# A spectral filter beside a gated MLP: the inverse transform's exchange is issued before its row and summed two pairs later, and the feature transform reads its low parts from a ninth tile

## The chip, the cores and the metric

The kernel runs on one core of a Trainium2 chip. The metric is the device time of one execution in microseconds (us), lower is better. One execution was taken by the hardware profiler; times inside it count from the start of its span. Engines: PE (matrix products, with PEld for its weight loads), DVE (vector), ACT (activations), POOL, and SP, whose queue issues every transfer here. Each engine takes its instructions in order.

## The reference

```python
x = A_x                                   # 1 x 2048 x 448, float32
xn = _layernorm(x, axis=-1)
X = jnp.fft.rfft2(xn, axes=(-2, -1))      # spectral branch
y = jnp.fft.irfft2(X * (w_r + 1j * w_i), s=(2048, 448), axes=(-2, -1))
gate = xn @ W_gate                        # 448 x 1792
up = xn @ W_up
h = gate * (gate > 0) * up                # gated branch
out = x + y + h @ W_down
```

## The kernel before, in words

All products run on PE in float16, each operand split into a high and a low part, so that one exact product costs three matmuls: high by high, high by low, low by high.

Tokens are held as 16 groups of 128 (`n2`), four groups to a chunk; chunks go in the order 0, 2, 1, 3. The 448 features are cut into four residues of 112. For a group, the normalized values stand in a tile `tt` of eight blocks of 128 columns: blocks 0 to 2 hold residues 0 to 2 with 16 values of residue 3 behind each; block 3 holds the last 64 values of residue 3, high part in its first half and low part in its second; blocks 4 to 6 hold the low parts of 0 to 2; block 7 gathers residue 3's high part, written by two POOL copies (`ln_copy`). The blocks are transposed into `Tq[q]`, for the first four groups by PE (`ln_tp`, `ln_ev`), for the others by one DMA transpose each (`ln_dma`).

**The gated branch** is the bulk of PE's work. Units `gu_unit` (L727, and half passes L734) make gate and up for 128 hidden columns by 512 tokens; `gu_post` brings them through ACT and DVE (`gu_relu` L764, `gu_times` L768, `gu_hi` L772, `gu_lo` L776); units `dn_mm` (L795) multiply by `W_down`, and `dn_post` (L801) adds to the result `xy`. Weights are scaled by a power of two found from a sum of squares (`w_sq` on ACT, `w_sum` an all-reduce on POOL, `w_scale`, then `w_hi` L677 and `w_lo` L681).

**The spectral branch** is a list of background steps (`bg`), dealt out between those units by a credit of DVE time. Forward: `f_dft` (L370) transforms a group over the features, `f_eo`, `f_x`, `f_lo` fold it, `f_sdft` (L412) transforms over 128 tokens with a table `fm`, and `stage2` to `stage4` finish over the 16 groups by DVE butterflies (L418 to L442). A real transform pairs each frequency with its mirror: `swap` sends the upper half of the partitions of two buffers to the lower half of an exchange tile `sw` and the lower half to the upper, by two transfers (L559, L560), and `pair` (L565, L566) adds or subtracts the tile. Three exchange tiles are used in turn. Then come the weights (`wmul`, from tiles `wf`), `turn`, and the inverse butterflies.

One frequency, partition 64 of the tiles, takes a separate way: `row_in` collects it into `row`, `row_hi` to `row_ev` transform it by two small products with `row_t`, and in the inverse half `i_swap` puts it back into partition 64 of the two buffers before it calls `swap`.

Inverse, for pair m = 0 to 7: `stage4`, `i_swap`, `i_pair`, `i_hi` and `i_lo` (L609, L615, into `vt`, two buffers), then for two groups each `i_sdft` (L625, table `im`), `i_pq` and `i_pqlo` (L631, L635, into `pgh`), `i_ddft` (L645) and `i_acc` (L650), which adds to `xy`; a group is stored (L807) when both branches have added to it. `i_sdft` and `i_ddft` share two PSUM banks `fx` with the other spectral products.

The order of the opening on every engine, up to the first chunk's hidden values and the first part of `W_down`, is written out by hand (`OPENING`, short names: `lo2` is `ln_lo` of group 2, `dm2` its `ln_dma`, `parW4` the all-reduce of weight tile 4). After it, each engine's order is set by a planner that simulates the program with priorities.

The lines that set the distance between exchange and sum: in the forward half

```python
if i0 < 8:
    add(bf[k0], stage4, k0, 1, "s3", "X")
if i0 > 1:
    add(1.26, pair, "X", ks[i0 - 2], 1)
if i0 < 8:
    add(0.0, swap, "X", k0)
```

and in the inverse half, for even half-steps t = 2m,

```python
if m < 8:
    add(bf[m], stage4, m, -1, "i3", "U")
if 0 <= m - 1 < 8:
    add(1.26, i_pair, m - 1)
    add(0.0, i_hi, m - 1)
if m < 8:
    add(0.0, i_swap, m)
```

Of the kernel before, what the change touches and what calls it, by code (L numbers as in the profile page):

```python
# [19 lines left out]
KC = 57  # L20
# [14 lines left out]
wloW0g1 lw lfd hh01 hh11 whiW1g0 st2 lh01 lh10 whiW1g1 hl01 wloW1g0 lw hl11 wsqW2g0 wloW1g1 lw ly0 ly4 ly8  # L35
ly12 lh11 wsqW3g0 st10 parW2 hp0 st14 wsqW3g1 gu1g0 st6 wdq0 parW3 wscW2 sqC wscW3 whiW2g0 rsC gu1g1 re0
wloW2g0 whiW3g1 tm0 whiW2g1 xn6 wsqW4g0 xn2 gu2g0 wloW2g1 hi2 re1 xn10 gh0 wloW3g1 whiW3g0 tm1 gu2g1 wdq1
wloW3g0 hi10 xn14 lo2 hi14 hi6 cp14 hp2 wsqW4g1 cp2 lo6 gu3g0 cp10 dm2 lo14 re2 parW4 wdq2 cp6 wscW4 tm2
whiW4g0 dm14 lo10 wdq4 gu3g1 wloW4g0 gh1 dm10 gl0 whiW4g1 gl1 dm6 gu4g0 re3 wloW4g1 wdq3 tm3 wdp gh3
# [30 lines left out]
def _fd_parts():  # L70

    names = [("h", r) for r in range(4)] + [("l", r) for r in range(4)] + [("x", 3)]
    off = {n: GW * i for i, n in enumerate(names)}
    for r in range(3):
        off["x", r] = GW * (9 + 2 * r)
    return off, GW * 15


# [8 lines left out]
def _constants():  # L87
    sc = 2.0 ** 10
    rows = _rows()
    kp = np.arange(KC)  # L90

    def dft(d):
        th = 2 * np.pi * ((np.outer(d, kp)) % D) / D
        return np.concatenate([np.cos(th), -np.sin(th)], axis=1) * sc

    off, width = _fd_parts()
    c_fd = np.zeros((128, width), np.float16)
    p = np.arange(128)
    in3 = (p < 48) | (p >= 64)
    d3 = 4 * np.where(p < 48, p, np.where(p < 64, 0, p - 16)) + 3  # L100
    for r in range(4):
        h, l = _split(dft(rows[r] if r < 3 else d3))
        keep = (p < 112 if r < 3 else in3)[:, None]
        c_fd[:, off["h", r]:off["h", r] + GW] = np.where(keep, h, 0)
        c_fd[:, off["l", r]:off["l", r] + GW] = np.where(keep, l, 0)
    for r in range(3):
        h, _ = _split(dft(rows[r]))
        c_fd[:, off["x", r]:off["x", r] + GW] = np.where((p < 112)[:, None], h, 0)
        c_fd[:, off["x", r] + GW:off["x", r] + 2 * GW] = np.where((p >= 112)[:, None], h, 0)
    h, _ = _split(dft(rows[3]))  # L110
    c_fd[:, off["x", 3]:off["x", 3] + GW] = np.where((p >= 64)[:, None], h, 0)
# [46 lines left out]
def tile_gfnet_reglu(ctx: ExitStack, tc: tile.TileContext, x, xr, wgu, wd, wf, wrow, ident, c_fd, c_fm, c_im, c_row, c_id,  # L158
# [19 lines left out]
    Tq = {q: mt([128, 8, 512], F16, f"T{q}") for q in CHUNKS}  # L178
# [9 lines left out]
    fd_off, fd_width = _fd_parts()  # L188
# [42 lines left out]
    fd_t = ft([128, fd_width], F16, "fd_t")  # L231
# [109 lines left out]
    def ln_dma(n2):  # L341
        q, j = n2 % 4, n2 // 4
        o = Tq[q][:, :, 128 * j:128 * (j + 1)]
        last["S"] = nc.sync.dma_start_transpose(o, tt[n2].rearrange("p a b -> p (a b)")).ins
# [18 lines left out]
    def f_dft(n2):  # L363
        q, j = n2 % 4, n2 // 4
        js = slice(128 * j, 128 * (j + 1))
        ps = fx()
        T = Tq[q]

        def mm(o, a, part, first=False):
            P.matmul(o, T[:, a, js], fd_t[:, fd_off[part]:fd_off[part] + (2 * GW if part in wide else GW)],  # L370
                     start=first, stop=True, skip_group_check=True)

        wide = [("x", r) for r in range(3)]
        p4 = ps[:, 0:4 * GW].rearrange("p (c w) -> p c w", c=4)
# [117 lines left out]
    def open_inv():  # L492
# [104 lines left out]
    def i_swap(m):  # L597
        for n in (m, m + 8):
            nc.sync.dma_start(cur["U", n][64:65].rearrange("p g c k -> p (g c) k"), row[8 * n:8 * n + 8, 0, :])
        swap("U", m)  # L600

# [217 lines left out]
    def ln_chunk(q):  # L819
# [14 lines left out]
    def fft_chunk(q):  # L834
        n = [q + 4 * j for j in (0, 2, 1, 3)]
        for t in range(10):
# [5 lines left out]
            for i, fn in steps + [(t - 1, f_eo), (t, f_dft)]:  # L842
# [4 lines left out]
                if fn is f_eo:  # L847
# [31 lines left out]
    add(0.0, lambda: nc.sync.dma_start(idc_t, c_id))  # L879
    ks = [0, 4, 2, 6, 1, 5, 3, 7]  # L880
# [161 lines left out]
    for c, q in enumerate(CHUNKS[:2]):  # L1042
# [114 lines left out]
def _arrays(A_x, A_w_r, A_w_i, B_W_gate, B_W_up, B_W_down):  # L1157
# [15 lines left out]
    wrow = wf[:, 64].reshape(16, 2, 4, 1, KC).repeat(2, axis=3).transpose(0, 2, 3, 1, 4).reshape(128, 2, KC)  # L1173
    wf = wf.reshape(2, 8, 128, 2, 4 * KC).transpose(1, 2, 3, 0, 4).reshape(8, 128, 16 * KC)
# [25 lines left out]
```

## Time and profile before

| | |
|---|---|
| median of 3 runs | 459.4 us (458.9 to 461.23) |
| the profiled execution | 459.03 us |
| its span | 457.2 us |
| PE busy | 440.9 us (96%) |
| DVE busy | 374.0 us (82%) |
| ACT, POOL busy | 177.6, 26.1 us |
| moved by DMA | 39.35 MB |

The span runs from the first to the last instruction; the 1.8 us by which the execution is longer lie around it. A group's idle time is that of its engine just before it, with what ended it; time that an engine off the chain sits idle costs nothing by itself.

### The profile page before, as it was taken

The page shows a single profiled execution, that of the slowest core. Times are in us where ns is not written, and L with a number is a line of the kernel's source. Part 1 is how long each engine was busy: PE and PEld are TensorE (multiplying, and loading weights), DVE is VectorE, ACT ScalarE, POOL GpSimd, SP SyncE. Part 2 cuts the span into 40 slices and gives each one's busy share as a digit, 9 for nine tenths or more (in the row PEclk, how much of TensorE's full clock was granted, in tenths as well). Part 3 has the DMA queues.
Part 4 walks back from the last instruction along what each step waited for, and adds up shares of the span by engine and source line. Part 5 has one row for each costly group of instructions (what it writes and reads, how often), then busy time and mean ns, then how long its engine had stood idle before and what let it go on. Part 6 is the DMA issues. An engine that isn't in the chain of part 4 may idle for free.

```text
span 457.2 us, 7054 instructions
## 1 busy us (share of the span) xinstructions
PE 440.9 (96%) x2618; PEld 220.3 (48%) x2618; DVE 374.0 (82%) x801; ACT 177.6 (39%) x363; POOL 26.1 (6%) x68
## 2 busy tenths in 40 slices
PE   7999999999999999999999999999999997989896
PEld 3544645544555444444444444444444454545464
DVE  5998798988759898999999997988886768665664
ACT  5996242522535573143224242642321341323220
POOL 2220030110000130000000000000000000000000
PEclk9999999999999999999999999999999999999999
DMA  7929992040002352350220210000002231121213
GB/s 257 355 49 288 309 260 57 10 108 1 1 24 94 106 173 80 83 161 1 83 81 1 69 55 0 1 0 0 2 3 80 67 91 44 38 93 53 94 53 115
DMA packets 36955, 39.35 MB, mean 86 GB/s; under 512 B 15878, under 2 KB 32184, under 8 KB 36920
## 3 DMA queue, kind: packets, MB, share of 16 engines
q1 hardware_dynamic: 36920, 38.89, 27.6%
q8 instruction: 20, 0.33, 0.3%
q14 instruction: 15, 0.12, 0.1%
HBM read 24.65 MB, written 3.67 MB: 62 GB/s over the span
## 4 chain that ended last, share of the span: by engine, by line
PE 78%; DVE 10%; DMA 7%; issue 2%; SPq 1%; ACT 1%; DVEq 0%; ACTq 0%
PE gu L727 45%; PE dn L795 23%; DMA sw<-y 5%; PE gu L734 3%; PE fx L370 3%; PE fx L412 2%; DVE vt L615 1%; DVE xy L801 1%; PE fx L645 1%; DMA y<-in_xr 1%; DVE g L768 1%; DVE y L565 1%; DVE y L566 1%; PE fx L625 1%; DVE xy L650 1%
## 5 line engine op out<-in xcount | busy, mean ns | idle before, releaser
L727 PE MATMUL gu<-T,wt 128*128 128x512 f16 (+1 forms) x1140 | 256.1, 375 | 0.0
L727 PEld LDWEIGHTS <-wt 128*128 128x128 f16 x1140 | 109.0, 98 | 129.6 <-issue 9.3
L795 PE MATMUL dn<-wdt,h 128*128 128x448 f16 x672 | 136.8, 352 | 1.4 <-DVE xy L801 1.4
L795 PEld LDWEIGHTS <-h 128*128 128x128 f16 x672 | 65.0, 98 | 61.7 <-issue 1.6
L764 ACT ACTIVATE g<-gu 128x512 f32<-128x512 f32 x56 | 33.3, 594 | 115.6 <-PE gu L734 81.6
L772 ACT ACTIVATE h<-g 128x512 f16<-128x512 f32 x56 | 34.9, 626 | 65.4 <-DVE g L768 65.3
L768 DVE SCALAR_TENSOR_TENSOR g<-gu,g 128x512 f32<-128x512 f32 x56 | 38.4, 685 | 12.4 <-ACT g L764 12.4
L801 DVE SCALAR_TENSOR_TENSOR xy<-dn,dsc,xy 128x448 f32<-128x448 f32 x48 | 32.6, 679 | 14.5 <-PE dn L795 14.2
L776 DVE TENSOR_TENSOR h<-g,h 128x512 f16<-128x512 f32 x56 | 38.3, 685 | 6.0 <-ACT h L772 5.8
L565 DVE TENSOR_TENSOR y<-y,sw 128x456 f32<-128x456 f32 x16 | 10.1, 630 | 22.2 <-DMA sw<-y 12.3
L677 ACT ACTIVATE wt<-wst,wsc 128x512 f16<-128x512 f32 x28 | 19.1, 714 | 14.7 <-DVE wsc L221 14.5
L681 DVE SCALAR_TENSOR_TENSOR wt<-wst,wsc,wt 128x512 f16<-128x512 f32 x28 | 20.2, 744 | 0.1
L734 PE MATMUL gu<-T,wt 64*128 64x512 f16 x112 | 17.0, 381 | 1.9 <-DVE g L768 1.7
L211 ACT ACTIVATE junk<-wst 128x512 bf16<-128x512 f32 x28 | 17.4, 622 | 0.4 <-DMA wst<-in_wgu 0.2
L214 POOL PARTITION_ALL_REDUCE wm<-wm x15 | 7.3, 489 | 166.7 <-ACT junk L211 166.7
L631 ACT ACTIVATE pgh<-fx 114x512 f16<-114x512 f32 x16 | 9.3, 588 | 17.4 <-PE fx L645 17.4
L419 DVE TENSOR_TENSOR y<-y 128x456 f32<-128x456 f32 x22 | 13.9, 631 | 2.6 <-DMA row<-y 2.3
L650 DVE SCALAR_TENSOR_TENSOR xy<-fx,fsc,xy 128x448 f32<-128x448 f32 x16 | 10.8, 680 | 6.2 <-PE fx L645 6.2
L625 PE MATMUL fx<-im,vt 128*128 128x128 f16 x192 | 13.2, 219 | 2.6 <-DVE xy L650 2.6
L609 ACT ACTIVATE vt<-y,fsc 128x912 f16<-128x912 f32 x8 | 8.4, 1051 | 18.0 <-DVE y L566 12.9
L625 PEld LDWEIGHTS <-vt 128*128 128x128 f16 x192 | 11.9, 98 | 6.6 <-issue 3.6
L645 PE MATMUL fx<-idc_t,pgh 114*128 114x112 f16 x192 | 11.9, 213 | 2.8 <-DVE pgh L635 2.8
(111 smaller groups left out, 426.5 us busy)
## 6 DMA issues: line engine op xcount, KB each, us to landing
sw<-y SPq DMA_DIRECT2D x32, 224.4 KB
wst<-in_wgu SPq DMA_DIRECT2D x28, 256.0 KB
wf<-in_wf SPq DMA_DIRECT2D x8, 456.0 KB
y<-in_xr SPq DMA_DIRECT2D x16, 224.0 KB
xy<-in_x SPq DMA_DIRECT2D x16, 224.0 KB
out<-xy SPq DMA_DIRECT2D x16, 224.0 KB
wdst<-in_wd SPq DMA_DIRECT2D x14, 224.0 KB
fm<-in_c_fm SPq DMA_DIRECT2D x16, 64.0 KB
```

What stands on the lines that cost most here:

```text
L211: A.activation(o, src, AF.Square, scale=SQ, accum_out=acc)
L625: P.matmul(o, v[:, h, w], m[:, c, :], start=(i == 0), stop=(i == 2), skip_group_check=True)
L677: A.activation(w[:, 0:4, :], wst[f, g], AF.Copy, scale=wsc[f, g])
L681: V.scalar_tensor_tensor(w[:, 4:8, :], st, sc, w[:, 0:4, :], op0=OP.mult, op1=OP.subtract)
L727: last["P"] = P.matmul(hps[f, q][:, g, cs], wt[f, g][:, a, :], Tq[q][:, b, cs], start=(start and i == 0), stop=(stop and i == len(seq) - 1 ...
L734: m = P.matmul(hps[f, q][:, g, 0:512], wt[f, g][rows, 7, :], Tq[q][rows, b, :], start=start, stop=not start).ins
L764: last["A"] = A.activation(g1s[f, q], hps[f, q][:, 0, :], AF.Relu, scale=2.0 ** -22).ins
L768: last["V"] = V.scalar_tensor_tensor(g1, hps[f, q][:, 1, :], 2.0 ** -22, g1, op0=OP.mult, op1=OP.mult).ins
L772: A.activation(ht[f, q][:, 0, :], g1s[f, q], AF.Copy)
L776: V.tensor_tensor(h[:, 1, :], g1s.pop((f, q)), h[:, 0, :], op=OP.subtract)
L795: last["P"] = P.matmul(ps[:, 0:D], ht[f, q][:, a, js], wdt[f][:, b, :], start=(i == 0), stop=(i == n - 1)).ins
L801: last["V"] = V.scalar_tensor_tensor(xy[:, n2, :], dps[n2][:, 0:D], dsc[:, g:g + 1], xy[:, n2, :], op0=OP.mult, op1=OP.add).ins
```

## The change

1. **Inverse exchange.** `i_swap` issues the two halves of the exchange first. The row then goes by one transfer, not two, into partition 64 of the exchange tile, not into the buffers. The buffers hold zero there (the weights' row 64 is set to zero, with its squares now taken by one more ACT step, `wsq_row`), so the pair's sum adds the row; the factor of i that the sum brings is put into the table `c_row`, and the order of `row`'s partitions is changed so that two buffers' rows lie together. The sum of pair m stands after `stage4` and `i_swap` of pair m + 2, not m + 1; what follows it moves with it.
2. **The ninth tile.** `tt` and `Tq` get a block 8, into which `ln_copy_lo` gathers residue 3's low part by two POOL copies per group. `f_dft` then makes, per residue, three products of 114 columns (12 in all); before it had eight of 114 columns, one of 114 and three of 228, which took the mixed blocks apart by tables with zero rows. The table `fd_t` shrinks from 1710 columns to 912. `ln_dma` moves nine blocks; for the first four groups, which PE transposes, block 8 alone goes by a DMA transpose (`dt`). In `OPENING`, steps `cl` (the copies) and `dt` are added.
3. **Tables.** `fm` and `im` are loaded for two groups at a time, eight loads for sixteen each. The inverse half's `im` (three pairs) and `pgh` (three buffers, two before) lie in the space of the `wf` tiles, which are free by then.

```diff
+dt0 dt4 wloW2g1 hi2 dt8 dt12 re1 ...          (OPENING, after gu2g0)
-wloW3g0 hi10 xn14 lo2 hi14 hi6 cp14 hp2 wsqW4g1 cp2 lo6 gu3g0 cp10 dm2 lo14 re2 parW4 wdq2 cp6 wscW4 tm2
-whiW4g0 dm14 lo10 wdq4 gu3g1 wloW4g0 gh1 dm10 gl0 whiW4g1 gl1 dm6 gu4g0 re3 wloW4g1 wdq3 tm3 wdp gh3
+wloW3g0 hi10 xn14 lo2 hi14 hi6 cp14 hp2 wsqW4g1 cp2 lo6 gu3g0 cp10 cl2 dm2 lo14 re2 parW4 wdq2 cp6 wscW4 tm2
+whiW4g0 cl14 dm14 lo10 wdq4 gu3g1 wloW4g0 gh1 cl10 dm10 gl0 whiW4g1 gl1 cl6 dm6 gu4g0 re3 wloW4g1 wdq3 tm3 wdp gh3
...
-    Tq = {q: mt([128, 8, 512], F16, f"T{q}") for q in CHUNKS}
+    Tq = {q: mt([128, 9, 512], F16, f"T{q}") for q in CHUNKS}
...
-        fm_t[n2] = ft([128, 2, 128], F16, "fm", 4)
+        fm_t[n2] = ft([128, 2, 2, 128], F16, "fm", 2)
...
+    def ln_copy_lo(n2):
+        t = tt[n2]
+        G.tensor_copy(t[:, 8, 0:48].rearrange("p (a b) -> p a b", b=16), t[:, 4:7, 112:128])
+        G.tensor_copy(t[:, 8, 64:128], t[:, 3, 64:128])
...
-    def ln_dma(n2):
+    def ln_dma(n2, a=0):
         q, j = n2 % 4, n2 // 4
-        o = Tq[q][:, :, 128 * j:128 * (j + 1)]
-        last["S"] = nc.sync.dma_start_transpose(o, tt[n2].rearrange("p a b -> p (a b)")).ins
+        o = Tq[q][:, a:9, 128 * j:128 * (j + 1)]
+        last["S"] = nc.sync.dma_start_transpose(o, tt[n2][:, a:9].rearrange("p a b -> p (a b)")).ins
...
-        for r in range(4):
-            a = r if r < 3 else 7
-            mm(ps[:, r * GW:(r + 1) * GW], a, ("h", r), r == 0)
-            mm(ps[:, r * GW:(r + 1) * GW], a, ("l", r))
-        mm(ps[:, 3 * GW:4 * GW], 3, ("x", 3))
-        for r in range(3):
-            mm(p4[:, r::3 - r, :], 4 + r, ("x", r))
+        for r in range(4):
+            a, b = (r, 4 + r) if r < 3 else (7, 8)
+            for i, (t, c) in enumerate(((a, 0), (a, 1), (b, 0))):
+                P.matmul(ps[:, r * GW:(r + 1) * GW], T[:, t, js], fd_t[:, r, c], start=(r == 0 and i == 0),
+                         stop=True, skip_group_check=True)
...
+    def wsq_row():
+        squares(roww.rearrange("p a b -> p (a b)"), small[:, 16:17])
...
+        state["wf"] = [ip.tile([128, 2, 2, 4, KC], F32, name=f"wf{i}") for i in range(3)]
+        spare = [w.rearrange("p a h b c -> p (a h b c)").bitcast(F16) for w in state["wf"]]
+        state["pgh"] = [w[0:GW, 0:1024].rearrange("p (a b c) -> p a b c", a=2, b=4) for w in spare]
+        state["im"] = [w[:, 1024:1536].rearrange("p (a b c) -> p a b c", a=2, b=2) for w in spare]
...
     def i_swap(m):
-        for n in (m, m + 8):
-            nc.sync.dma_start(cur["U", n][64:65].rearrange("p g c k -> p (g c) k"), row[8 * n:8 * n + 8, 0, :])
         swap("U", m)
+        nc.sync.dma_start(sw["U", m][64:65].rearrange("p n g c k -> p (n g c) k"), row[16 * m:16 * m + 16, 0, :])
...
-    for t in range(16 + 4 + len(il)):
+    for t in range(16 + 6 + len(il)):
         m = t // 2
         if t % 2 == 0:
             if m < 8:
                 add(bf[m], stage4, m, -1, "i3", "U")
-            if 0 <= m - 1 < 8:
-                add(1.26, i_pair, m - 1)
-                add(0.0, i_hi, m - 1)
-            if m < 8:
                 add(0.0, i_swap, m)
-        elif 0 <= m - 1 < 8:
-            add(1.1, i_lo, m - 1)
-        if 3 <= t < 19:
-            add(0.0, load_im, io[t - 3])
+            if 0 <= m - 2 < 8:
+                add(1.26, i_pair, m - 2)
+                add(0.0, i_hi, m - 2)
+            if 0 <= m - 2 < 8:
+                add(0.0, load_im, m - 2)
+        elif 0 <= m - 2 < 8:
+            add(1.1, i_lo, m - 2)
         for st in reversed(range(len(il))):
-            i = t - 4 - st
+            i = t - 6 - st
...
+    wf[:, 64] = 0
```

More of the change, by code (lines that the diff above doesn't have):

```diff
@@ L67, in _cols @@
     return np.concatenate([m + r for r in (0, 2, 1, 3)]), np.concatenate([*_rows()[:3], _rows()[3, :64]])
-def _fd_parts():
-    names = [("h", r) for r in range(4)] + [("l", r) for r in range(4)] + [("x", 3)]
-    off = {n: GW * i for i, n in enumerate(names)}
-    for r in range(3):
-        off["x", r] = GW * (9 + 2 * r)
-    return off, GW * 15
 def _freqs():
@@ L94, in dft @@
         return np.concatenate([np.cos(th), -np.sin(th)], axis=1) * sc
-    off, width = _fd_parts()
-    c_fd = np.zeros((128, width), np.float16)
+    c_fd = np.zeros((128, 4, 2, GW), np.float16)
     p = np.arange(128)
@@ L101, in _constants @@
     for r in range(4):
-        h, l = _split(dft(rows[r] if r < 3 else d3))
         keep = (p < 112 if r < 3 else in3)[:, None]
[L104 to L111, printed above, removed]
+        for i, w in enumerate(_split(dft(rows[r] if r < 3 else d3))):
+            c_fd[:, r, i] = np.where(keep, w, 0)
     n1 = np.arange(128)
     k1 = np.where(n1 <= 64, n1, n1 - 64)
-    c_fm = np.zeros((16, 128, 2, 128), np.float16)
-    c_im = np.zeros((16, 128, 2, 128), np.float16)
+    c_fm = np.zeros((8, 128, 2, 2, 128), np.float16)
+    c_im = np.zeros((8, 128, 2, 2, 128), np.float16)
     for n2 in range(16):
@@ L120, in _constants @@
         w[:, 64] = (-1.0) ** n1
-        c_fm[n2] = np.stack(_split(w * sc), axis=1)
-        c_im[n2] = np.stack(_split(w.T * sc), axis=1)
+        c_fm[n2 % 8, :, n2 // 8] = np.stack(_split(w * sc), axis=1)
+        c_im[n2 % 8, :, n2 // 8] = np.stack(_split(w.T * sc), axis=1)
     r = np.arange(16)
@@ L137, in _constants @@
     c_row = []
-    for z in (np.einsum("ar,gh->agrh", m, own), np.einsum("ar,gh,g->agrh", 1j * m, own, sign),
-              np.einsum("ra,gh->rgah", back, turn)):
+    at = np.arange(16).reshape(2, 8).T.reshape(-1)
+    for z in (np.einsum("ar,gh->agrh", m[at], own), np.einsum("ar,gh,g->agrh", 1j * m[at], own, sign),
+              np.einsum("ra,gh->rgah", -1j * back[:, at], turn)):
         w = real(z).transpose(0, 1, 4, 2, 3, 5).reshape(128, 128)
@@ L230, in tile_gfnet_reglu @@
     id_t = ft([128, 128], F16, "id_t")
-    fd_t = ft([128, fd_width], F16, "fd_t")
+    fd_t = ft([128, 4, 2, GW], F16, "fd_t")
     warm = ft([128, 512], F16, "warm")
@@ L298, in tile_gfnet_reglu @@
     xn, tt, xn_b = {}, {}, {}
-    tts = [ft([128, 8, 128], F16, f"tt{i}") for i in range(4)]
+    tts = [ft([128, 9, 128], F16, f"tt{i}") for i in range(4)]
     for t in tts:
-        G.memset(t[:, 7, 48:64], 0.0)
+        G.memset(t[:, 7:9, 48:64], 0.0)
     def new_tt(n2):
@@ L367, in f_dft @@
         T = Tq[q]
[L369 to L374, printed above, removed]
-        for r in range(4):
-            a = r if r < 3 else 7
-            mm(ps[:, r * GW:(r + 1) * GW], a, ("h", r), r == 0)
-            mm(ps[:, r * GW:(r + 1) * GW], a, ("l", r))
-        mm(ps[:, 3 * GW:4 * GW], 3, ("x", 3))
-        for r in range(3):
-            mm(p4[:, r::3 - r, :], 4 + r, ("x", r))
+        for r in range(4):
+            a, b = (r, 4 + r) if r < 3 else (7, 8)
+            for i, (t, c) in enumerate(((a, 0), (a, 1), (b, 0))):
+                P.matmul(ps[:, r * GW:(r + 1) * GW], T[:, t, js], fd_t[:, r, c], start=(r == 0 and i == 0),
+                         stop=True, skip_group_check=True)
         zps[n2] = ps
@@ L476, in wsq @@
             squares(w[:, :, h].rearrange("p a b c -> p a (b c)"), small[:, k + 8 * h:k + 8 * h + 1])
+    def wsq_row():
+        squares(roww.rearrange("p a b -> p (a b)"), small[:, 16:17])
     def wsq_fin():
-        V.tensor_reduce(small[:, 16:17], small[:, 0:16], axis=AX.X, op=OP.add)
-        all_sum(small[:, 17:18], small[:, 16:17])
+        V.tensor_reduce(small[:, 21:22], small[:, 0:17], axis=AX.X, op=OP.add)
+        all_sum(small[:, 17:18], small[:, 21:22])
     def wsq_scale():
@@ L569, in row_in @@
         for par in range(2):
-            n = j + 8 * par
-            nc.sync.dma_start(row[8 * n:8 * n + 8, 0, :],
-                              cur["s1", j, par][64:65].rearrange("p g c k -> p (g c) k"))
+            p = 16 * j + 8 * par
+            nc.sync.dma_start(row[p:p + 8, 0, :], cur["s1", j, par][64:65].rearrange("p g c k -> p (g c) k"))
     def row_hi(sc):
@@ L629, in i_pq @@
         ps = sps[n2]
-        pgh[n2] = it([GW, 2, 4, 128], F16, "pgh", 2)
+        pgh[n2] = state["pgh"][state.setdefault("pn", 0) % 3]
+        state["pn"] += 1
         A.activation(pgh[n2][:, 0].rearrange("p a b -> p (a b)"), ps[0:GW, :], AF.Copy, scale=2.0 ** -14)
@@ L846, in fft_chunk @@
                 add(cost, fn, n[i])
-                if fn is f_eo:
+                if fn is f_eo and i in (0, 2):
                     add(0.0, load_fm, n[i])
@@ L879, in tile_gfnet_reglu @@
     add(0.0, lambda: nc.sync.dma_start(idc_t, c_id))
+    add(0.0, wsq_row)
     ks = [0, 4, 2, 6, 1, 5, 3, 7]
```

20 lines of the change are left out of this document (11 added, 9 removed).

## The prediction

> **What bounds the kernel now.** I began with the page's engines, cut the span into stages, and read the stage that loses PE time row by row: PE's timeline, DVE's waits, the chain.
>
> ```profile
> PE 440.9 (96%) x2618; PEld 220.3 (48%) x2618; DVE 374.0 (82%) x801; ACT 177.6 (39%) x363; POOL 26.1 (6%) x68
> ```
> ```profile
> 0.00:22.86 22.86, 18.80 (x119) 10.14 (x120) 17.38 (x62) 16.55 (x37) 4.91 (x22) 1.00 0.89 306
> 22.86:160.00 137.14, 137.14 (x810) 68.96 (x809) 114.89 (x270) 65.03 (x134) 13.74 (x35) 1.00 0.38 109
> 160.00:343.00 183.00, 183.00 (x906) 83.47 (x905) 167.94 (x348) 66.75 (x148) 7.41 (x12) 1.00 0.17 50
> 354.33:434.34 80.01, 71.50 (x544) 39.78 (x541) 54.28 (x92) 23.52 (x37) 0.00 (x0) 1.00 0.22 69
> 434.34:453.50 19.16, 19.15 (x186) 12.48 (x184) 11.19 (x18) 3.50 (x6) 0.00 (x0) 1.00 0.22 78
> 453.50:457.20 3.70, 0.00 (x0) 0.00 (x0) 0.68 (x1) 0.00 (x0) 0.00 (x0) 0.86 0.31 115
> ```
>
> The columns after the length are PE, PEld, DVE, ACT and POOL busy. PE is the bound, at a granted clock of 1.00: from 22.86 to 343 it has no gap. It loses 4.06 us while the first data arrive, 3.70 us at the end (last store), and 80.01 − 71.50 = 8.51 us between 354 and 434, the inverse transform. So two things can move the time: fewer PE cycles in the gapless stretches, and those 8.51 us. PE's timeline (start, length, idle before and its releaser) gives the gaps one by one:
>
> ```profile
> 366.20 0.61 PE L734 MATMUL gu<-T,wt 64*128 64x512 f16 x4 [0.74 <-DVE g L768]
> 380.57 0.83 PE L625 MATMUL fx<-im,vt 128*128 128x128 f16 x12 [1.71 <-DVE xy L650]
> 382.84 0.73 PE L795 MATMUL dn<-wdt,h 128*128 128x448 f16 x3 [1.44 <-DVE xy L801]
> 406.36 0.61 PE L734 MATMUL gu<-T,wt 64*128 64x512 f16 x4 [0.94 <-DVE g L768]
> 422.22 0.83 PE L625 MATMUL fx<-im,vt 128*128 128x128 f16 x12 [0.90 <-DVE xy L650]
> 424.49 0.75 PE L645 MATMUL fx<-idc_t,pgh 114*128 114x112 f16 x12 [1.44 <-DVE pgh L635]
> ```
>
> These make 7.17 us; two smaller ones before L645 the rest. DVE releases every one, yet DVE has 25.7 us idle in that stage. Its waits, for that stage and then for 160 to 343, and one exchange out of the chain, say why:
>
> ```profile
> DVE y L565 <- DMA sw<-y: 10.6, 3, 4.4
> DVE y L565 <- issue: 9.6, 3, 3.4
> ...
> DVE y L565 <- DMA sw<-y: 1.7, 1, 1.7
> ```
> ```profile
> 371.08 0.31 DVE y L428
> ...
> 372.00 0.26 SPq L599
> ...
> 372.31 0.84 SPq L559
> ...
> 373.20 4.82 DMA sw<-y
> ...
> 378.14 0.63 DVE y L565
> 378.78 0.55 DVE y L566
> ...
> 380.51 1.08 DVE vt L615
> ...
> 391.96 0.63 DVE y L565
> ```
>
> After `stage4` (L428 or L442) SP issues two row transfers (L599), then both halves of the exchange, and the second half lands 4.82 us after its issue. The pair's sum L565 stands early in DVE's in-order queue, so everything PE needs from DVE (g, pgh, xy) stands behind it: 20.2 us of DVE waiting in the stage, of which PE feels 8.51.
>
> **The change, part by part.**
>
> **Exchange first, sum two pairs later.** In the forward half `pair` already follows its `swap` by two pairs, with the same three buffers: eight exchanges, one DVE wait of 1.7 us, and PE at 183.00 of 183.00 us. The inverse takes that distance. The exchange then needs 0.84 for the first issue and 4.82 from the second, 5.7 us, while two further `stage4`, one older sum and all g, h, xy work stand between. The successive sums here start at 378.14 and 391.96, 13.8 us apart with 4.4 us of waiting in it, so more than 9 us for one pair of distance and some 18 for two. What would be late next is the inverse chain itself (matmul, pgh, matmul, xy, with two `fx` banks). The row 434.34:453.50 tells its size: the same L625 and L645 matmuls with no exchange left, and PE busy 19.15 of 19.16. DVE, at 54.28 of 80.01, would be at 54.28 of 71.5, or 76%. Bounds: 8.51 us recovered, or none if other DVE lateness takes its place. I take 8.0, near the forward half's row, and leave 0.5 for a stray gap. In SP's queue each pair loses one of its row issues, and the row goes behind the exchange, off its path. Pair m+3's exchange reuses pair m's buffer, whose sum precedes `stage4` of m+3 on DVE: no new wait.
>
> **Fourier matmuls over the feature axis (`f_dft`).** Before: 8 of 114 columns, one of 114, three of 228, 1710 in all; after: 12 of 114, 1368. Weight loads stay at 12.
>
> ```profile
> 54.26 1.50 PE fx L370 x24
> 436.89 0.59 PE fx L645 x12
> 442.40 0.67 PE fx L625 x12
> ```
> ```profile
> L370 PEld LDWEIGHTS <-T 128*128 128x128 f16 x192 | 11.8, 97 | 2.6 <-issue 0.8
> ```
>
> 24 take 1.50 us, 0.75 for one token group, 0.439 ns a column. L645 and L625, twelve of 112 and 128 columns with a weight load each, run at 0.44 too, so narrowness costs nothing here: 1368 columns make 0.60 us, 0.15 saved, times 16 = 2.4 us, all in stretches where PE has no gap. The other end: if the load (97 ns, hidden until now) set the pace, 12 × 97 = 1.16 us, 0.41 more, +6.6 us in all. I take −2.4.
>
> The Trainium skill, page "TensorE: Matmul & The Clock Gate", section "Back-to-back issue gap", speaks against this part: it gives about 81 ns a matmul at 128 columns in a stream of load and matmul pairs. By it a group would take 12 × 81 = 0.97 us, 0.22 more than now, or +3.5 us over 16 instead of −2.4. The trace disagrees: L625's twelve at 128 columns take 0.67 us, 56 ns each.
>
> **The ninth tile.** Each group gets two more POOL copies and a transpose of nine tiles for eight; the first four groups one more transpose each (`dt`), which SP can issue where it now has nothing, between the rows at 17.58 and 30.27. Only the opening is tight, around 31 us:
>
> ```profile
> 30.18 0.22 POOL L324 COPY tt<-tt 128x48 f16<-128x48 f16 x1
> 30.35 0.56 POOL L325 COPY tt<-tt 128x64 f16<-128x64 f16 x1
> 30.89 0.40 POOL L214 PARTITION_ALL_REDUCE wm<-wm  x1
> ...
> 61.31 2.72 POOL L325 COPY tt<-tt 128x64 f16<-128x64 f16 x1
> ```
> ```profile
> 32.81 0.74 DVE L681 SCALAR_TENSOR_TENSOR wt<-wst,wsc,wt 128x512 f16<-128x512 f32 x1
> ...
> 29.27 8.81 PE L727 MATMUL gu<-T,wt 128*128 128x512 f16 x40
> 38.54 4.49 PE L727 MATMUL gu<-T,wt 128*128 128x512 f16 x20
> 76.41 5.99 PE L727 MATMUL gu<-T,wt 128*128 128x512 f16 x27
> ...
> 17.58 2.77 SPq L239 DMA_DIRECT2D xy<-in_x  x4
> 30.27 5.41 SPq L344 DMA_TRANSPOSE T<-tt  x4
> 69.38 1.25 SPq L344 DMA_TRANSPOSE T<-tt  x1
> ...
> 36.50:37.00 0.50, 0.50 (x4) 0.20 (x2) 0.43 (x3) 0.50 (x2) 0.00 (x0) 1.00 0.38 86
> ```
>
> `cl2` goes ahead of the all-reduce of the fifth weight tile, and DVE, ACT and PE hang on that in a row. A pair of copies takes 30.89 − 30.18 = 0.71 us here. The reduce then lets `wloW4g0` end at 33.55 + 0.71 = 34.26, and PE wants it with the 22nd matmul of the row at 29.27, at 33.9: a stall of up to 0.4. The transposes start 0.7 later and take 9/8 of 5.41, ending near 37.1 for 35.7; their traffic now fades about 1.1 us after the last issue (the 86 GB/s row), so 38.2, just ahead of 38.54. Bounds: 0, and 2.7 − 0.3 = 2.4 if a copy is held as long as the one at 61.31. I take +0.2, nearest the rows at 30.2. In the later chunks the copies lengthen the way to the transpose by 0.7 us; the third chunk's last transpose is issued by 70.63, and its first matmul comes after the second chunk's five units of twenty; 80 of that hundred are done by 76.41 and the row there has the last twenty, so it starts near 80.8: hidden by some 9 us.
>
> The Trainium skill, page "SBUF — State Buffer", section "Who interferes with whom", says that a DVE instruction with two SBUF inputs contends with a GpSimd instruction that reads SBUF, and the loser blocks. The 2.72 us copy agrees with it; by it `cl2` could be held for as long as DVE's run of subtractions, the upper bound above.
>
> **The rest, at nothing.** Half as many `fm` and `im` loads of twice the size: SP is mostly idle, and an `im` pair is now issued two or more half-steps ahead of its matmul instead of one. `fd_t` shrinks from 1710 columns to 912 and is used first by L370, long after it has come. A third `pgh` buffer takes a wait away, if any. One more Square and its accumulator read on ACT, 0.9 us by the mean of ACT's instructions from 160 to 343 (66.75 / 148), lie in the 116 us that ACT is idle there; without that cover they would delay one g by as much.
>
> **Sum.** The profiled execution took 459.03 us: its span of 457.2 and 1.8 around it; the median of the runs shown is 459.4, 0.4 above. 459.03 − 8.0 − 2.4 + 0.2 = 448.8, as a median 449.2.
>
> **The rivals.** (A) Half of the inverse's gaps stay or come back, because DVE's in-order bursts and not only the exchange make g and pgh late (for: every gap names DVE; against: 434 to 453.5). Then 4.3 return: 453.5. (B) All stay, and only the columns count: 449.2 + 8.0 = 457.2.
>
> (C) The other side: an `im` load delays PE. It is now issued behind the exchange and the row in SP's queue, and nothing hides it if PE's order puts its matmul straight behind the pair's own work. The pair's two sums and its L615 are 0.63 + 0.55 + 1.08 = 2.3 us of cover; a load that lands like half an exchange (4.8 us) would leave 2.5 us, eight times 20, less the 10.2 gained: 469. It decides from 10.2 / 8 = 1.3 us a load. Against it: `im` was as late before, and no wait for it stands in the trace.
>
> (D) Weight loads pace the narrow matmuls: 449.2 + 2.4 + 6.6 = 458.2.
>
> (E) The opening stalls by its upper bound: 449.2 + 2.2 = 451.4.
>
> **How the numbers follow.** Forecast 0.53 (448 to 450.5), E 0.10, A 0.20, B 0.09, D 0.03, C 0.05. Two runs that differ by under 0.5% (2.3 us) can't be told from no change here. Forecast, E and A are faster by more (0.83); B lies on that edge at 457.2 and is split, so faster 0.87, same 0.08, slower 0.05. The range reaches from 447.6 (both gains whole, 459.03 − 10.9 = 448.1, less some scatter) to 454.5, just past A; about 0.17 lies outside.
>
> **What the next profile would show.** Right: no DVE wait of more than 2 us at the pair's sum after 343, PE gaps between 340 and the last matmul under 1.5 us in all, L370's 24 matmuls in 1.2 us with no 228-column form, and PE without a gap from 31 to 40. Wrong: gaps there behind g, pgh or xy with DVE busy (A, B), behind `im` or SP (C), L370 still at 0.75 us a group (D), or a stall near 34 behind the scaled weights (E).

## The result, and the profile after

The changed kernel takes 448.57 us, the median of four runs (448.32 to 448.9); the kernel before, run beside it, 460.09 (458.9 to 461.23). The ratio is 0.975, with a 95% interval of 0.9721 to 0.978. The profiled execution took 448.66 us, its span 446.9. New line numbers: the exchange is issued by L547 and L548, the sums are L553 and L554, `i_lo` is L601, `f_dft` L360, `i_sdft` L611, `i_ddft` L632, `gu_unit` L714 and L721, `gu_times` L755, `dn_mm` L782, the transposes L332, the copies L307 and L308, for the ninth block L312 and L313. `pgh` now lies in the space of `wf` and bears that name.

The page's line for PE, then the windows of the stages (length, then busy time of PE, PEld, DVE, ACT and POOL):

```profile
PE 437.4 (98%) x2618; PEld 217.6 (49%) x2618; DVE 373.0 (83%) x801; ACT 178.7 (40%) x365; POOL 35.5 (8%) x100
```
```profile
22.86:160.00 137.14, 136.38 (x816) 67.37 (x815) 114.48 (x270) 66.88 (x138) 20.96 (x59) 1.00 0.40 113
160.00:343.00 183.00, 183.00 (x908) 83.42 (x906) 168.16 (x350) 65.78 (x147) 7.48 (x12) 1.00 0.16 52
343.00:434.34 91.34, 90.53 (x698) 51.17 (x697) 67.13 (x114) 28.74 (x44) 0.00 (x0) 1.00 0.22 71
```

In the inverse transform PE now idles 91.34 − 90.53 = 0.81 us, for 8.51 before. The stretch from 22.86 to 160, which had no gap, has lost 137.14 − 136.38 = 0.76. PE's timeline has one gap in each of the two:

```profile
29.12 8.99 PE L714 MATMUL gu<-T,wt 128*128 128x512 f16 x40
38.87 0.61 PE L721 MATMUL gu<-T,wt 64*128 64x512 f16 x4 [0.75 <-DMA T<-tt]
...
49.35 1.38 PE L360 MATMUL fx<-fd_t,T 128*128 128x114 f16 x24
50.57 5.08 PE L782 MATMUL dn<-wdt,h 128*128 128x448 f16 x26
...
399.49 0.61 PE L721 MATMUL gu<-T,wt 64*128 64x512 f16 x4 [0.81 <-DVE g L755]
```

The row at 29.12 is longer than before's 8.81 with the same forty matmuls: a wait of 0.2 us inside it. Two groups of `f_dft` start at 49.35 and the next matmul at 50.57, so 24 matmuls take 1.22 us of PE's time, for 1.50 before. The groups of the page show that all have 114 columns:

```profile
L360 PE MATMUL fx<-fd_t,T 128*128 128x114 f16 x192 | 11.4, 213 | 0.0
```

DVE's waits at the pair's sum, over the window from 343 to 446, and the two that are left, as the timeline of DVE shows them with the `i_lo` and the `stage4` between:

```profile
DVE y L553 <- DMA sw<-y: 7.3, 2, 4.3
```
```profile
384.89 0.63 DVE L553 TENSOR_TENSOR y<-y,sw 128x456 f32<-128x456 f32 x1 [2.99 <-DMA sw<-y]
...
387.18 1.16 DVE L601 SCALAR_TENSOR_TENSOR vt<-y,fsc,vt 128x912 f16<-128x912 f32 x1
...
388.85 0.39 DVE L415 SCALAR_TENSOR_TENSOR y<-y 128x228 f32<-128x228 f32 x1
...
397.66 0.63 DVE L553 TENSOR_TENSOR y<-y,sw 128x456 f32<-128x456 f32 x1 [4.27 <-DMA sw<-y]
```

So 20.2 us of waiting at the sum became 7.3, and PE feels 0.81 of it: the `g` that releases the half pass at 399.49 stands behind the sum at 397.66. The two waits belong to the last two pairs. Before 397.66 the exchange could only be issued after the `stage4` that starts at 388.85, and that one stands behind the `i_lo` at 387.18.

The chain of waits across the opening shows where the new 0.75 us comes from: the copies, one after another on POOL, then the transposes' landing.

```profile
31.10 0.40 POOL wm L197
...
31.80 0.68 DVE g L755
32.49 0.47 DVE tt L323
...
33.18 0.70 POOL tt L313
33.88 0.63 POOL tt L312
34.51 0.64 POOL tt L313
35.15 0.30 issue
35.45 3.28 DMA T<-tt
38.73 0.14 issue
38.87 0.61 PE gu L721 x4
```

The spans differ by 457.2 − 446.9 = 10.3 us: 7.7 from the gaps of the inverse transform, 0.14 × 16 = 2.24 from `f_dft`, less 0.95 for the opening's two waits. That leaves 1.3. Most of it fits the way the timeline counts a row's end: the 24 matmuls at 49.35 are drawn as 1.38 us while the next matmul starts after 1.22, so 0.16 us of a last matmul overlap its successor, and ahead of a gap they overlap nothing and count as busy. Of the inverse's eight gaps seven went, and the opening has one more: 6 × 0.16 = 1.0. Besides, the row at 29.12 starts 0.15 sooner than before's, at 29.27, and the span ends 3.60 us behind PE's last matmul, before 3.76. This is a reading of rows; no run took it apart.

### The profile page after: what moved, and what is told of

It reads as the page before. It is cut to its first block, busy times and chain, and to the rows that moved or that the text cites. A ratio compares the mean times of both kernels' runs of the same rounds, so it can differ in the third digit from the quotient of the medians.

```text
span 446.9 us, 7057 instructions
## 1 busy us (share of the span) xinstructions
PE 437.4 (98%) x2618; PEld 217.6 (49%) x2618; DVE 373.0 (83%) x801; ACT 178.7 (40%) x365; POOL 35.5 (8%) x100
## 4 chain that ended last, share of the span: by engine, by line
PE 84%; DVE 7%; DMA 4%; ACT 1%; issue 1%; POOL 1%; SPq 1%; DVEq 0%; ACTq 0%
PE gu L714 47%; PE dn L782 27%; PE gu L721 3%; PE fx L360 2%; PE fx L392 2%; DMA sw<-y 2%; PE fx L611 2%; PE fx L632 1%; DMA y<-in_xr 1%; DVE g L755 1%; DMA T<-tt 1%; DVE bst L256 1%; DVE wt L668 1%; DVE xy L788 1%; DVE y L553 1%
## 5 line engine op out<-in xcount | busy, mean ns | idle before, releaser
L714 PE MATMUL gu<-T,wt 128*128 128x512 f16 (+1 forms) x1140 | 256.1, 376 | 0.0
L714 PEld LDWEIGHTS <-wt 128*128 128x128 f16 x1140 | 108.6, 98 | 129.9 <-issue 9.3
L782 PE MATMUL dn<-wdt,h 128*128 128x448 f16 x672 | 136.4, 352 | 0.0
L782 PEld LDWEIGHTS <-h 128*128 128x128 f16 x672 | 64.8, 98 | 60.5
L755 DVE SCALAR_TENSOR_TENSOR g<-gu,g 128x512 f32<-128x512 f32 x56 | 38.3, 684 | 10.3 <-ACT g L751 10.2
L788 DVE SCALAR_TENSOR_TENSOR xy<-dn,dsc,xy 128x448 f32<-128x448 f32 x48 | 32.5, 678 | 15.5 <-PE dn L782 15.3
L763 DVE TENSOR_TENSOR h<-g,h 128x512 f16<-128x512 f32 x56 | 38.2, 684 | 4.9 <-ACT h L759 4.8
L721 PE MATMUL gu<-T,wt 64*128 64x512 f16 x112 | 17.0, 381 | 1.7 <-DVE g L755 0.8
L399 DVE TENSOR_TENSOR y<-y 128x456 f32<-128x456 f32 x22 | 13.9, 630 | 4.7 <-DMA row<-y 4.5
L553 DVE TENSOR_TENSOR y<-y,sw 128x456 f32<-128x456 f32 x16 | 10.0, 626 | 8.5 <-DMA sw<-y 8.5
L618 ACT ACTIVATE wf<-fx 114x512 f16<-114x512 f32 x16 | 9.4, 587 | 17.2 <-PE fx L611 17.0
L398 DVE TENSOR_TENSOR y<-y 128x456 f32<-128x456 f32 x22 | 13.8, 626 | 0.2
L611 PEld LDWEIGHTS <-vt 128*128 128x128 f16 x192 | 12.0, 98 | 3.3
L611 PE MATMUL fx<-wf,vt 128*128 128x128 f16 x192 | 13.2, 219 | 0.0
```

Source lines behind the costliest of these rows:

```text
L611: P.matmul(o, v[:, h, w], m[:, c, :], start=(i == 0), stop=(i == 2), skip_group_check=True)
L714: last["P"] = P.matmul(hps[f, q][:, g, cs], wt[f, g][:, a, :], Tq[q][:, b, cs], start=(start and i == 0), stop=(stop and i == len(seq) - 1 ...
L721: m = P.matmul(hps[f, q][:, g, 0:512], wt[f, g][rows, 7, :], Tq[q][rows, b, :], start=start, stop=not start).ins
L755: last["V"] = V.scalar_tensor_tensor(g1, hps[f, q][:, 1, :], 2.0 ** -22, g1, op0=OP.mult, op1=OP.mult).ins
L763: V.tensor_tensor(h[:, 1, :], g1s.pop((f, q)), h[:, 0, :], op=OP.subtract)
L782: last["P"] = P.matmul(ps[:, 0:D], ht[f, q][:, a, js], wdt[f][:, b, :], start=(i == 0), stop=(i == n - 1)).ins
```

## The experiments

Each experiment was timed beside the kernel before, whose medians lay between 459.0 and 460.25 us; the ratios are to it.

**1. The changed kernel again**, as the base for the next three.

> The changed kernel once more, beside the three that follow. 448.6 us; PE gaps of 0.75 us at the first half pass on the second chunk (released by the transpose) and of 0.8 us near 399 us (behind g).

448.71 us (448.45 to 449.37), ratio 0.9767 (0.9741 to 0.9793).

**2. The scratch buffer that was freed longest ago.** The planner had put the last two sums ahead of the next `stage4`, which takes its buffer from a list whose last entry `i_lo` had just freed.

```diff
+        if sgn < 0:
+            free.append(free.pop(0))
         cur[dst, k], cur[dst, k + 8] = bfly(a, b, k, sgn)
```

> In the changed kernel, the inverse stage4 takes its scratch buffer from the old end of the free list, not the one that i_lo freed last. Theory: the last two exchanges still hold DVE (7.3 us) because stage4 of pairs 6 and 7 waits for the buffer that i_lo of pairs 3 and 4 frees, so that it and its exchange come only just ahead of the sum; with an older buffer stage4 runs ahead, DVE's waits at the pair's sum fall under 1 us in all, and the PE gap of 0.8 us near 399 goes: 447.7 us. Rival: the order is the planner's alone, or vt's two buffers hold the sums anyway: waits of some 7 us and 448.6 us as before.

448.66 us (448.51 to 448.71), ratio 0.9762 (0.9737 to 0.9786). The waits of the window 340 to 460 and the row of 343 to 441, first of the kernel of experiment 1, then of this one:

```profile
DVE y L553 <- DMA sw<-y: 7.0, 2, 4.1
```
```profile
343.00:441.00 98.00, 97.49 (x771) 55.93 (x769) 71.06 (x120) 29.35 (x45) 0.00 (x0) 1.00 0.22 74
```
```profile
DVE y L555 <- DMA sw<-y: 2.0, 2, 1.7
```
```profile
343.00:441.00 98.00, 97.66 (x771) 56.02 (x770) 70.64 (x120) 29.89 (x45) 0.00 (x0) 1.00 0.22 74
```

The cause of the two waits is shown: with an older buffer 5.0 of 7.0 us go. The gain that I expected of it fell: PE's idle time went from 0.51 to 0.34, and the time did not move. Of what DVE waits there, hardly anything was on PE's path.

**3. The ninth blocks later.** The second chunk's transposes in the opening move eight blocks and do not wait for the low copies, the all-reduce goes ahead of `cl2`, and four transposes of one block each follow outside the opening.

```diff
-... cp10 cl2 dm2 lo14 re2 parW4 wdq2 cp6 wscW4 tm2
+... cp10 dm2 lo14 re2 parW4 wdq2 cp6 cl2 wscW4 tm2
-    def ln_dma(n2, a=0):
+    def ln_dma(n2, a=0, b=9):
...
+    for j in (0, 3, 2, 1):
+        add(0.0, ln_dma, CHUNKS[1] + 4 * j, 8)
```

> In the changed kernel, the second chunk's four opening transposes move eight blocks and do not wait for the copies into the ninth; the ninth blocks go by four transposes of their own as the first background steps, and the all-reduce of the fifth weight tile goes ahead of the first of those copies. Theory: the new PE gap of 0.75 us is the last nine-block transpose landing late for the first half pass on the second chunk, and 0.2 us more is the all-reduce behind the copies; both go: 447.7 us. Rival: a transpose of one block holds SP about as long as one of eight (1.18 for 1.25 us), so four more put 4.7 us into SP's queue ahead of the next loads, and PE waits there: 448.6 to 451 us.

447.48 us (447.18 to 447.77), ratio 0.9736 (0.9711 to 0.9762): 1.2 us less than in experiment 1, and the fastest kernel of all. Its opening stage is without a gap again, the row of forty matmuls is back at 8.81 us, and the four added issues cost PE nothing (window, then SP's timeline):

```profile
22.86:160.00 137.14, 137.14 (x821) 67.86 (x820) 115.44 (x274) 66.73 (x139) 20.68 (x60) 1.00 0.42 117
```
```profile
38.88 6.09 SPq L332 DMA_TRANSPOSE T<-tt  x4
```

**4. Both.**

> Both edits together. Theory: the gaps stand in different stages, so the gains add: 446.8 us, PE gaps under 0.3 us between the opening and the last matmul. Rival: one of them shifts work onto the other's place: no better than the better of the two.

447.6 us (447.49 to 447.69), ratio 0.9739 (0.9714 to 0.9764): the same as experiment 3, since the oldest buffer brings nothing. My 446.8 fell.

**5 to 8. The change taken apart.** 5 has the new exchange with the feature transform of before, 6 the ninth tile with the exchange of before (row first, sum one pair later). 7 and 8 have the ninth tile and one half of the exchange's change each: 7 issues the exchange first, with the row through the exchange tile, and sums one pair later, 8 sends the row first, by two transfers into the buffers, and sums two pairs later. The edits of 7 and 8; 6 has both, with `i_swap` behind `i_pair` again:

```diff
(7)
-    for t in range(16 + 6 + len(il)):
+    for t in range(16 + 4 + len(il)):
...
-            if 0 <= m - 2 < 8:
-                add(1.26, i_pair, m - 2)
+            if 0 <= m - 1 < 8:
+                add(1.26, i_pair, m - 1)
...
-            i = t - 6 - st
+            i = t - 4 - st
(8)
+        for par in range(2):
+            p = 16 * m + 8 * par
+            nc.sync.dma_start(cur["U", m + 8 * par][64:65].rearrange("p g c k -> p (g c) k"), row[p:p + 8, 0, :])
         swap("U", m)
-        nc.sync.dma_start(sw["U", m][64:65].rearrange("p n g c k -> p (n g c) k"), row[16 * m:16 * m + 16, 0, :])
```

> The changed kernel with the feature transform of before: eight blocks, tables of 1710 columns, no copies into a ninth tile. Theory: the exchange part alone closes the inverse's PE gaps, 7.7 us and some 1.2 us of matmul tail that counts as busy ahead of each gap: 459.0 - 8.9 = 450.1 us. Rival: the two parts depend on each other and the exchange alone gains less than 7 us: above 452.

> The changed kernel with the inverse exchange of before: row first into the two buffers, sum one pair later. Theory: feature transform -2.3 us, opening +0.9 us: 459.0 - 1.4 = 457.6 us, with PE gaps of about 8.5 us in the inverse. Rival: the later im loads or the third pgh buffer closed the gaps: under 453.

> The changed kernel with the sum one pair later, as before the change; exchange first and row through the exchange tile stay. Theory (distance): the exchange is only some 1.4 us sooner for each pair, so about half of DVE's 20 us of waiting stays, and with it 4 us of PE gaps: 452.8 us (451 to 455). Rival (order): getting the two row issues out of the exchange's way was the gain: 448.7 us, as the changed kernel.

> The changed kernel with the row sent first, by two transfers into the two buffers, as before the change; the sum stays two pairs later. Theory (distance): the longer way is hidden where the distance holds and costs 1.4 us of DVE waiting at the last two pairs: 448.7 to 449.8 us. Rival (order): back near 457 us.

| | us | ratio to before |
|---|---|---|
| 5, exchange alone | 451.01 (450.9 to 451.56) | 0.9813 (0.979 to 0.9836) |
| 6, ninth tile alone | 458.14 (457.46 to 459.25) | 0.9963 (0.9947 to 0.9979) |
| 7, order alone, one pair | 453.05 (452.0 to 453.37) | 0.9851 (0.9826 to 0.9876) |
| 8, row first, two pairs | 449.72 (448.94 to 452.32) | 0.9776 (0.9748 to 0.9803) |

The window from 343 to 441 of the kernel before, then of 6, 7 and 8; PE's busy time of 98.00 is the third number:

```profile
343.00:441.00 98.00, 89.48 (x671) 49.72 (x670) 65.07 (x110) 27.26 (x43) 0.00 (x0) 1.00 0.21 68
```
```profile
343.00:441.00 98.00, 89.56 (x661) 49.28 (x660) 63.84 (x109) 26.79 (x42) 0.00 (x0) 0.98 0.20 63
```
```profile
343.00:441.00 98.00, 93.31 (x712) 52.33 (x710) 68.40 (x115) 28.40 (x44) 0.00 (x0) 1.00 0.21 69
```
```profile
343.00:441.00 98.00, 95.74 (x735) 53.94 (x733) 68.92 (x116) 29.55 (x45) 0.00 (x0) 0.98 0.22 72
```

Their waits at the sum, from 340 on, in the same order for 6, 7 and 8:

```profile
DVE y L553 <- DMA sw<-y: 15.3, 4, 4.7
...
DVE y L553 <- issue: 4.9, 3, 2.9
```
```profile
DVE y L553 <- DMA sw<-y: 11.7, 5, 3.9
...
DVE y L553 <- issue: 4.2, 2, 2.2
```
```profile
DVE y L553 <- DMA sw<-y: 9.4, 3, 5.0
```

The exchange is worth 459.71 − 451.01 = 8.7 us, the ninth tile 459.71 − 458.14 = 1.6; their sum, 10.3, is 0.8 short of the 11.1 between that median of before and 448.6. That is within the scatter of the runs of before (458.3 to 461.2), but the profile of 5 also shows a place for it: from 160 to 343, where the kernel before and the changed kernel have no gap, PE loses 0.90 us, ahead of the matmuls at 193.73 (0.48) and 202.03 (0.42). What in the planned order makes these two gaps was not tested.

```profile
160.00:343.00 183.00, 182.10 (x901) 82.97 (x899) 167.63 (x348) 67.24 (x150) 7.47 (x12) 1.00 0.17 51
```

6 has the later `im` loads and the third `pgh` buffer, and still 98.00 − 89.56 = 8.44 us of PE's gaps: the third part of the change does not close them. From 458.14, the order alone brings 5.1 us, the distance alone 8.4, both together (448.57) 9.6. So the two are not terms of a sum but two ways to the same gaps, and the distance alone is nearly enough. The profile of 8 is of a run of 452.12, near the upper end of its six. Its 98.00 − 95.74 = 2.26 us of idle time are one gap, ending at 401.35, and behind it the trace has PE at a granted clock of 0.50 for 3.4 us, by an estimate another 1.7 us lost. So it says little of the median. My rivals that let the order decide alone, 448.7 for 7 and some 457 for 8, fell, and so did the one for 6, under 453.

**9. Eight blocks, the order as changed.** Experiment 3 without the line of the opening's order, to split the 0.75 us.

```diff
-    def ln_dma(n2, a=0):
+    def ln_dma(n2, a=0, b=9):
...
+    for j in (0, 3, 2, 1):
+        add(0.0, ln_dma, CHUNKS[1] + 4 * j, 8)
```

> The opening's order stays that of the changed kernel, the low copies (cl) ahead of the transposes' places included, but the second chunk's four transposes move eight blocks again, and block 8 of its groups follows by four small transposes outside the opening. Question: is the gap of 0.75 us at 38.87, where PE waits for a transposed tile, due to the late issue of the transposes or to their ninth block? Theory late: the transposes are issued as late as now, from 31.1 to about 35.4, so a wait for T stays near 38 with 0.4 us or more, and the 0.2 us near 34 behind the scaled weights stays too: 448.0 to 448.5. Rival size: nine blocks are what lands late; with eight the wait for T goes and only the 0.2 us stay: 447.6.

447.85 us (447.71 to 448.29), ratio 0.9753 (0.9712 to 0.9794). SP's timeline of the changed kernel and of this one:

```profile
31.14 5.63 SPq L332 DMA_TRANSPOSE T<-tt  x4
```
```profile
29.57 5.97 SPq L332 DMA_TRANSPOSE T<-tt  x4
```

It did not tell the two apart. Transposes of eight blocks no longer need the low copies, so the first went out 1.57 us earlier, which "as late as now" had ruled out. The wait for the transposed tile went. The 0.2 us behind the scaled weights stayed, as both had said: the row of forty matmuls is as long as in the changed kernel.

```profile
28.89 8.99 PE L714 MATMUL gu<-T,wt 128*128 128x512 f16 x40
```

So shown is that the ninth block, with the wait for the copies that fill it, cost the 0.75. The traces allow an estimate of the two shares. The last transpose landed at 38.73 in the changed kernel and at 37.40 here, 1.33 us sooner; its issue ended at 36.77 and at 35.54, 1.23 sooner, and took 1.96 and 1.86 from there to the landing. Eight blocks issued as late as the nine, at 35.45, would have landed at 35.45 + 1.25 + 1.86 = 38.56, which is 0.17 sooner. By this most of the gap is the lateness; no run shows it.

**10 to 12. What slows the transposes' traffic?** In the slices of half a microsecond around 32 to 36 the transposes moved up to 290 GB/s before, 195 to 217 in full slices of the changed kernel, and no more than 218 in experiments 3 and 9, where they have eight blocks (last column; 32 to 32.5 of the kernel before, of experiment 5, then 36 to 36.5 of the changed kernel):

```profile
32.00:32.50 0.50, 0.50 (x4) 0.20 (x2) 0.50 (x2) 0.50 (x2) 0.00 (x0) 1.00 1.27 286
```
```profile
32.00:32.50 0.50, 0.50 (x4) 0.23 (x3) 0.50 (x2) 0.50 (x2) 0.00 (x0) 1.00 1.27 289
```
```profile
36.00:36.50 0.50, 0.50 (x4) 0.26 (x3) 0.47 (x3) 0.15 (x1) 0.20 (x1) 1.00 1.13 195
```

Three versions of experiment 3 put the ninth block into a tile of its own, on the source side (`tt`), on the destination side (`Tq`), and on both, so that the tiles of the eight-block transposes are as they were before. For both:

```diff
-    Tq = {q: mt([128, 9, 512], F16, f"T{q}") for q in CHUNKS}
+    Tq = {q: mt([128, 8, 512], F16, f"T{q}") for q in CHUNKS}
+    Tn = {q: mt([128, 512], F16, f"Tn{q}") for q in CHUNKS}
...
-    tts = [ft([128, 9, 128], F16, f"tt{i}") for i in range(4)]
+    tts = [ft([128, 8, 128], F16, f"tt{i}") for i in range(4)]
+    t9s = [ft([128, 128], F16, f"tn{i}") for i in range(4)]
```

> The late-ninth kernel with the ninth block of each group's normalized values in a tile of its own: the source of the eight-block transposes is again a tile of eight blocks, 2048 bytes a partition, as in the kernel before; their destination keeps nine. Every later group's ninth block is a second transpose. Question: the eight-block transposes moved 204 to 218 GB/s in full slices with nine-block tiles, 286 to 291 before. Theory source pitch: 285 to 291 again here, and about 210 in the run with only the destination apart. Rival destination pitch: still 205 to 220 here. Rival neighbours (the added copies on POOL slow the traffic, not the layout): 205 to 220 in both runs around 31 to 37. Time by all of them: 447.5, within 0.7, since no PE time waits there any more.

> The late-ninth kernel with the ninth block of each chunk's transposed values in a tile of its own: the destination of the eight-block transposes is again a tile of eight blocks, as before; their source keeps nine blocks, 2304 bytes a partition. Theory source pitch: about 205 to 220 GB/s in full slices. Rival destination pitch: 285 to 291. Rival neighbours: 205 to 220 in both runs. Time by all: 447.5, within 0.7.

> Both halves at once: the ninth block of the source and that of the destination each in a tile of its own, so an eight-block transpose reads and writes tiles of eight blocks, as in the kernel before. With one side apart the full slices stayed at 200 to 220 GB/s. Theory layout: a nine-block tile on either side is enough to slow the transposes, and 285 to 291 come back here. Rival not the layout: 200 to 220 here too, and what slows them (the added copies, or where the tiles lie) stays open. Time: 447.5 if the third chunk is not delayed, up to 450.7 if it waits again as with the source apart, where each later group's ninth block is a second transpose.

450.65 us (449.23 to 451.67), 449.02 (448.69 to 451.16) and 450.33 (448.48 to 451.32); ratios 0.9795 (0.9767 to 0.9824), 0.9777 (0.9744 to 0.9811) and 0.9801 (0.977 to 0.9832). The transposes' traffic stayed under 225 GB/s in all three, as in this row of the last:

```profile
36.00:36.50 0.50, 0.50 (x4) 0.24 (x3) 0.43 (x5) 0.40 (x1) 0.00 (x0) 1.00 1.14 210
```

So the layout is not it, and neither is POOL at that moment, which is idle in that row. The traces show what the lower rate is made of. The four opening transposes of eight blocks are 4096 packets of 256 bytes. In the kernel before and in experiment 5 each of these took 18 ns; in experiments 3 and 9 to 12 between 447 and 475 of them, one in nine, took over 30 ns, 43 in the mean, and so did 562 of the changed kernel's 4608. The changed kernel's last two transposes, from 98.91 to 101.92, where POOL has no work, have 267 such packets among 2304; the kernel before has none from 94 to 100. Experiment 5 has the old feature transform and the old rate, so it comes with the second part of the change; what in it does that, where the tiles lie or something else, stays open.

My 447.5 for the first two times fell, by 3.2 and 1.5 us; the third lies within the 447.5 to 450.7 that I gave it. Each later group then has two transposes, each of which holds SP for about 1.2 us, and with the source apart PE waits for the third chunk (PE's timeline):

```profile
81.96 1.89 PE L722 MATMUL gu<-T,wt 128*128 128x512 f16 x8 [2.60 <-DVE bst L256]
```

The releaser named there is a guess of the profile; SP's last transpose of that chunk is issued at 79.95. With both apart the gap is 0.21 us in the profiled run, and with the destination apart there is none; these runs, at 448.48 and 448.69, are the lowest of their four, so the medians of 450.33 and 449.02 are not explained by such a wait.

## Why the prediction was right, point by point

**The inverse gaps, −8.0.** Right in size and cause. PE's gaps fell by 7.7 us, by 8.8 if the ends of the rows ahead of them are counted (7 × 0.16), and experiment 5 gave 8.7 for this part. The step behind it was only partly right. I reckoned with some 18 us between exchange and sum for two pairs of distance and said that no DVE wait over 2 us would be left; two were left, 2.99 and 4.27, because the planner let the last two `stage4` wait for a buffer. PE felt 0.81 of these 7.3 us, which the prediction had not separated: what counts is whether g, `pgh` and `xy` are late, and experiment 2 removed 5 us of DVE's waiting for no time at all. The row from which I took the size, PE without a gap once no exchange was left, was the better guide than the waits.

**`f_dft`, −2.4.** Right: 0.61 us a group, 0.60 forecast, −2.24 in all. A matmul of 114 columns took 1.22 / 24 us = 51 ns. By the 81 ns at 128 columns of the Trainium skill, page "TensorE: Matmul & The Clock Gate", section "Back-to-back issue gap", the part would have cost time; the trace disagrees with it in both kernels. Experiment 6, the ninth tile alone, gave −1.6, which is −2.24 and the opening's 0.95, −1.3, within its scatter.

**The opening, +0.2.** Wrong: 0.95, and PE was not without a gap from 31 to 40. The stall behind the scaled weights, "up to 0.4", was 0.2 and well bounded. Two other steps failed. I let the last transposes land at 38.2, "just ahead of 38.54", the row of the full matmuls. The first reader of the second chunk is the half pass ahead of them, as before's chain of waits shows:

```profile
29.33 8.74 PE gu L727 x40
38.07 0.54 PE gu L734 x4
38.61 1.40 PE gu L727 x6
```

So the forecast landing was already 0.1 too late, for nothing in my sum. And I took the end of the traffic, read off the row with 86 GB/s, for the moment at which PE can read the tile. In the trace the transposes' last packet ends at 38.20, just as forecast, but the landing comes 0.53 later, at 38.73, and PE's matmul at 38.87; in the kernel before the last packet ends at 36.73 and the landing comes at 37.19. That 38.20 itself came out was in part luck: the last issue ended at 36.77, for 37.1 forecast, and the traffic took 1.43 from there, for 1.1. The last copies took 0.7 us each, where the prediction had a pair at 0.71; the 2.72 us of the upper bound did not come. POOL's and DVE's timelines of the changed kernel, first a copy while DVE is idle (28.91 to 29.54), then one beside an instruction of DVE with two inputs:

```profile
29.04 0.22 POOL L307 COPY tt<-tt 128x48 f16<-128x48 f16 x1 [7.33 <-ACT tt L303]
...
33.82 0.68 POOL L312 COPY tt<-tt 128x48 f16<-128x48 f16 x1
```
```profile
33.70 1.34 DVE L763 TENSOR_TENSOR h<-g,h 128x512 f16<-128x512 f32 x2
```

A copy of the same shape takes three times as long there. That agrees with the Trainium skill, page "SBUF — State Buffer", section "Who interferes with whom", by which two such instructions contend and the loser blocks.

**The rest, at nothing.** No wait of PE for an `im` load (its tile bears the name `wf` too) stands anywhere in the waits of the whole span, so rival C has nothing for it. 160 to 343 is as full as it was.

**The sum.** 448.8 forecast for the profiled execution, 448.66 measured. It is closer than its terms, by luck: 0.75 us too little for the opening, 0.3 too much for the gaps and 0.16 too much for `f_dft` stand against the 1.3 that the rows' ends, the earlier start and the shorter end gave, for which the sum had no term.

**The rivals.** A fell: the one gap left in the inverse stands behind a sum that waited for its exchange, not behind a burst of DVE. Experiment 7 comes close to A's 453.5, at 453.05, and its largest gaps name `pgh`, as A said, but that does not test A: with one pair of distance the sums still waited 15.9 us for their exchanges, and how much of the 4.69 us of gaps these waits make, and how much DVE's order, was not taken apart. B's gaps went. D fell with the 51 ns. E's mechanism was there but small: copies were held to 0.7 us, a quarter of its 2.72, and the stall behind the weights was 0.2, for its 2.4.

## What to carry to other kernels

A wait in an in-order queue is worth only what the bottleneck engine loses behind it: here 13 us less of DVE's waiting brought some 8, and the next 5 nothing, so size such a change by PE's gaps and not by the waits. When a transfer is given one more source, everything that reads it waits for the latest one; find the first reader in the timeline, half passes too, count to the landing and not to the end of the traffic (0.5 us between them here), and if the stretch is tight, send the new piece by itself, later (experiment 3, −1.2 us, with the all-reduce's place, some 0.2 of it). Where two edits attack the same gaps, as order and distance do, do not add their gains.

## What the runs showed of the hardware

A DMA transpose of one, eight or nine blocks of 128 × 128 holds SP's queue for almost the same time: 1.18, 1.25 and 1.32 us (medians; twelve of the last row's sixteen have nine). These are the transposes of the changed kernel from 19 to 28 us, with one block each, then all of before, then all of the changed kernel (minimum, median and maximum in ns):

```profile
L332 SPq DMA_TRANSPOSE T<-tt x4: 1162/1182/1206, 20.2 to 24.1; - x4
```
```profile
L344 SPq DMA_TRANSPOSE T<-tt x12: 1231/1252/1362, 30.3 to 97.6; - x12
```
```profile
L332 SPq DMA_TRANSPOSE T<-tt x16: 1162/1317/1383, 20.2 to 99.1; - x16
```

A split transpose thus costs its queue another 1.2 us; in experiment 3 the four one-block issues took 6.09 us in all, 1.5 each. And transposes of eight blocks from and to tiles of the same shape moved 286 to 291 GB/s in full slices in one kernel and 195 to 220 in another. The difference is one packet in nine, which took 43 ns where the others took 18, for a reason that three runs did not find. Last, the end of a transfer's traffic is not its landing: 0.46 and 0.53 us lay between the two for the last opening transposes of before and of the changed kernel.
